# A residual block of a diffusion model: broken and unbroken PSUM writes in the plain products, and an opening cut in halves

## The chip, the cores and the metric

The kernel runs on one core of one Trainium2 chip. The metric is the time of one execution on the device, in microseconds (us), as the median of several runs. A core has five engines that the text names: TensorE (PE, matrix products; PEld is its loading of weights), VectorE (DVE), ScalarE (ACT), GpSimd (POOL) and SyncE (SP, which here only issues DMAs). Products land in PSUM, eight banks of 512 fp32 values in each of 128 partitions; DVE and ACT read them from there into SBUF.

## What is computed

Two images of 512 channels and 64 x 64 pixels go through group norm, silu and a 3 x 3 convolution, twice, with a time embedding added between, and the input added at the end:

```python
    h = conv3(_silu(gn(x, g1, be1)), w1)
    emb = _silu(t_emb) @ w_emb
    h = h + emb.reshape(B, C, 1, 1)
    h = conv3(_silu(gn(h, g2, be2)), w2)
    return x + h
```

`gn` has four groups of 128 channels, so that a group is exactly one block of 128 partitions; `conv3` pads with zeros and sums nine taps.

## The kernel before

**Tiling.** Channels are four blocks of 128 (`ct` for the input, `k` or `j` for the output). The work is eight chunks: layer 0 or 1, image 0 or 1, upper or lower half of the rows. A chunk has four units, one for each output block. A row of 64 pixels is stored as 32 even columns, one zero, 32 odd columns, so rows have a pitch of 65 elements (`RW`), and a plane (`PL`) has 8 rows.

**Fast convolution.** The rows of the 3 x 3 window are not multiplied one by one. Input rows are combined into six planes `s` (planes 4 and 5 by `rows_a`, planes 0 to 3 by `rows_b`, sums and scalings on DVE or ACT), each plane is multiplied with row-combined weights (`row_w`, called by `prep_w1` and `prep_w2`), and a unit combines the six results to output rows. Along columns a plane is either multiplied with the three column taps (`plain_mms`: products of 512 columns, 3 taps for each of 4 input blocks, all summed in one bank), or reduced once more along columns (`B_mms`, `A_mms`: products of 256 columns). Chunk 0 uses only plain products, chunks 1 to 3 use them for planes 1, 3, 4 and 5, chunks 4 to 6 for planes 4 and 5, chunk 7 for none: 1152 plain products and 1536 of width 256 in all.

**A plain product's patterns** (lines 780 to 791). The side taps (`kx` 0 and 2) read a plane as 8 runs of 64 elements and write the bank with the two halves of each row exchanged: `Ps(bank, 32, [[64, 8], [-32, 2], [1, 32]])`. The centre tap (`kx` 1) reads 16 runs of 32 elements and writes the bank without a break. `evac_o` and `evac_m` (lines 930 to 935) then read the bank without a break, on ACT.

**Order.** The kernel is not written in the order in which it runs. Every step is an operation with an engine, a price in us, and the memory it reads and writes; a planner (`Plan`) derives the dependences, simulates the five queues with these prices, and issues each engine's instructions in the order of that simulation. Within an engine the order is fixed from then on. `solve` makes priorities from the lengths of the paths behind each operation and then adds a list of seeded random offsets (`ORDER`); `boost` and `push` shift single operations.

**The opening** (lines 1120 to 1245). The first image's norm needs its statistics before any product can run. `stats0(ct)` takes them for one block: each half of the image by one of three ways, `CFG['st0']`: on DVE (`bn`: statistics instructions, their aggregation, two small steps), on ACT (a squaring with an accumulator, the sum by products with ones), or on PE. `gn_chain` sums over partitions by small fp32 products, then five small steps on DVE and a power on POOL (line 527) give scale and bias (lines 529 and 531). `silu` on ACT applies both to all 33 rows, `rows_a` makes planes 4 and 5 together, and their products for three output blocks (`opening`, banks 0 to 5) run while the other blocks' norms are made. Then come `rows_b`, the remaining products of unit 0, and the chunks. The row-combined weights of output block 0 and input block 0 are made on PE (`pe_w1`): 12 products with scaled identities (made by POOL, line 1201) and one evacuation. The other blocks' weights are made by `prep_w1` (two scalings on ACT, three 768-wide sums on DVE).

**Other parts touched.** `emb` makes the embedding on PE out of five loads of `w_emb`. `stats1` takes the second image's statistics on ACT during chunk 0. In a unit's end, `CFG['s']` names the engine of three scalings for each chunk (line 1019). `last_y` (line 1056) is the very last unit's end, on DVE.

Of the kernel before, what the change touches and what calls it, by code (L numbers as in the profile page):

```python
# [21 lines left out]
class Op:  # L22
    __slots__ = ("i", "eng", "cost", "lat", "fn", "preds", "succs", "name", "start", "slack", "sw", "boost")


ORDER = (2, (
    (194738957, 20, 15, 0.3),
    (101069860, -50, 500, 0.3),
    (792247291, 256, 60, 0.3),
    (343585110, 429, 120, 0.3),  # L30
    (204379228, 255, 30, 1),
    (228258273, 205, 30, 0.3),
    (909785710, 175, 15, 3),
    (736748984, 341, 30, 3),
    (920935792, 232, 15, 1),
    (771920438, 148, 30, 0.3),
    (603830373, 185, 60, 1),
    (465507377, 35, 15, 3),
    (12286073, 156, 15, 3),
    (538606607, 42, 15, 0.3),  # L40
    (581003105, 181, 60, 0.3),
    (15050380, 351, 120, 0.3),
    (657287205, 50, 30, 1),
    (104726034, 137, 60, 1),
    (1026753447, 57, 15, 0.3),
    (567570243, -16, 30, 1),
    (655024064, 49, 30, 0.3),
    (871214791, 61, 30, 3),
    (1017425442, 337, 30, 1),
    (41879747, 157, 120, 0.3),  # L50
    (6871566, 68, 15, 1),
    (894584394, 172, 15, 1),
    (297107780, 183, 60, 0.3),
    (207024721, 173, 60, 0.3),
    (908214038, 37, 30, 1),
    (122425277, 28, 30, 0.3),
    (791595493, 332, 15, 1),
    (223803721, 57, 15, 1),
    (904223640, 360, 15, 3),
    (301944938, 170, 120, 1),  # L60
    (380912920, 352, 60, 0.3),
    (625742557, 201, 30, 1),
    (907392232, 310, 15, 1),
    (117292907, 217, 60, 0.3),
    (948785046, 259, 15, 1),
    (731252551, 400, 15, 3),
    (676749781, 361, 15, 1),
    (521842705, 215, 60, 0.3),
    (955098089, 181, 15, 0.3),
    (956556455, 137, 15, 1),  # L70
# [3 lines left out]
class Plan:  # L74
# [118 lines left out]
    def solve(self, rounds=3):  # L193
# [15 lines left out]
        st, span = self._run(pris[k], False)  # L209
        st, pri = np.array(st), np.array(pris[k])  # L210
# [33 lines left out]
def _idx(off, dims):  # L244
# [27 lines left out]
    's': ((A_, A_, A_), (D_, D_, D_), (D_, A_, A_), (D_, D_, D_), (A_, A_, A_), (A_, A_, A_), (A_, A_, A_), (D_, A_, D_)),  # L272
    'oacc': (1,1,1,0,0,0,0,0),
    'np': 1,
    'st0': ('DA', 'DA', 'DP', 'PP'),
    'st1': 'AAAA',
    'warm': 9,
    'push': (40.0, 0.0, 0.0, 0.0),
    'wpe': (1, 0, 0, 0),
# [5 lines left out]
def kernel(  # L285
# [112 lines left out]
    def tt(out, a, b, op, name=""):  # L398
        pl.op("DVE", 0.075 + 0.000521 * out.n, lambda: nc.vector.tensor_tensor(out=out.ap, in0=a.ap, in1=b.ap, op=op),  # L399
              regs(a, b), regs(out), name)  # L400
# [5 lines left out]
    def act(out, a, func, scale=1.0, bias=None, acc=None, name=""):  # L406
        kw = {}
        rr, ww = [a], [out]
        sc = scale
        if isinstance(scale, R):  # L410
            rr.append(scale)
            sc = scale.ap
        if bias is not None:
            rr.append(bias)
            kw["bias"] = bias.ap
        if acc is not None:
            ww.append(acc)
            kw["accum_out"] = acc.ap
        if out.ap.dtype == F8:
            kw["saturate"] = False  # L420
        pl.op("ACT", (0.05 if a.reg[0] == "P" else 0.1) + 0.000833 * out.n + (0.09 if acc is not None else 0.0) + (0.18 if bias is not None else 0.0),
              lambda: nc.scalar.activation(out=out.ap, in_=a.ap, func=func, scale=sc, **kw), regs(*rr), regs(*ww), name)  # L422
# [18 lines left out]
    def mm(lst, name="", chain=True, slack=2.5, boost=0.0, warm=1.0):  # L441
        rr, ww, cost = [], [], 0.0
        for out, lhsT, rhs, st, sp in lst:
            rr += [lhsT, rhs]
            ww.append(out)
            cost += {512: 0.2222, 256: 0.109, 384: 0.166}.get(rhs.n, max(0.0715, rhs.n / 2330.0)) * warm
# [27 lines left out]
    EPSC = Fc(CT)  # L474

# [12 lines left out]
    nc.vector.memset(fs[:, EPSC:EPSC + CT], EPS)  # L488
    nc.gpsimd.tensor_tensor(out=fs[:, WARM:WARM + 1], in0=fs[:, WARM + 1:WARM + 2], in1=fs[:, NEGH:NEGH + 1], op=ALU.pow)
# [11 lines left out]
    def small(fn, r, w, name, cost=0.125):  # L501
        pl.op("DVE", cost, fn, regs(*r), regs(*w), name)

    def gn_chain(layer, b, ct, mes, name, SB=7, slack=5.0, n=1):
# [6 lines left out]
        lst.append((Ps(SB, n, [[1, n]]), cneg, F(EPSC, n), False, True))  # L511
# [6 lines left out]
        pl.op("DVE", 0.16, lambda: V.tensor_copy(out=F(tot, 2 * n).ap, in_=ps.ap), regs(ps), regs(F(tot, 2 * n)), name, boost=bo)  # L518
# [3 lines left out]
        else:  # L522
# [3 lines left out]
              [N], [N], name)  # L526
        pl.op("POOL", 0.85 if n == 1 else 1.9, lambda: nc.gpsimd.tensor_tensor(  # L527
            out=F(rs, n).ap, in0=N.ap, in1=F(NEGH, n).ap, op=ALU.pow), regs(N), regs(F(rs, n)), name)
        small(lambda: V.tensor_mul(out=S.ap, in0=F(rs, n).ap, in1=F(g, n).ap), [F(rs, n)], [S], name)
        if n == 1:  # L530
            small(lambda: V.scalar_tensor_tensor(  # L531
# [156 lines left out]
    def silu(c, ct):  # L688
        l, b, ch = chunks[c]
        ab = acur[(c, ct)]  # L690
        r0 = RW if ch == 0 else 0
        dims = [[RW, 33], [33, 2], [1, 32]]
# [6 lines left out]
    def rows_a(c, ct, w, keng, early):  # L699
# [10 lines left out]
        else:  # L710
            tt(v45, two(w, 0, 25), two(ab, 9, 17), SB_, nm)

# [63 lines left out]
    def plain_mms(bank, c, k, ct, s):  # L776
# [3 lines left out]
        for i, kx in enumerate((0, 2, 1)):  # L780
# [6 lines left out]
            if kx == 1:  # L787
                rhs, o = A(vo, [[RW, 8], [33, 2], [1, 32]]), Ps(bank, 0, [[1, 512]])
            else:
                rhs, o = A(vo + kx // 2, [[RW, 8], [1, 64]]), Ps(bank, 32, [[64, 8], [-32, 2], [1, 32]])  # L790
# [113 lines left out]
    def unit(c, k, opening=0):  # L904
# [25 lines left out]
        def evac_o(s, bank):  # L930
            act(A(OO[s - 4], [[RW, 8], [33, 2], [1, 32]]), Ps(bank, 0, [[1, 512]]), fid,
                scale=(0.25, 1.0)[s - 4], acc=acc(s), name=nm + f"o{s}")

        def evac_m(s, bank, i):
            act(M(s), Ps(bank, 0, [[1, 512]]), fid, scale=KAP[s], acc=i, name=nm + f"m{s}")

        def evac_pair(s, bank):
            act(M(s, 2, 1024), Ps(bank, 0, [[512, 2], [1, 512]]), ACT.Copy, scale=KAP[s], name=nm + f"m{s}")

# [43 lines left out]
        elif md == "0":  # L983
# [9 lines left out]
            evac_m(2, p2, acc(1))  # L993
            evac_m(0, p2 + 1, None)
# [61 lines left out]
    def last_y(c, k, M, SD, OS, OA, bank):  # L1056
# [16 lines left out]
        ts(M(1), M(0), 2.0, nm + "2")  # L1073
        tt(row(yb, 8, BF16), one(dx + 512), M(1), AD, nm + "y")
        ts(M(3), M(2), 4.0, nm + "4")
# [5 lines left out]
        ts(M(1), M(0), 8.0, nm + "8")  # L1081
# [48 lines left out]
    def bn(pieces, out, scale, name):  # L1130
        mv = Fc(2)
        V = nc.vector
        for i, d in enumerate(pieces):
# [6 lines left out]
        small(lambda: V.tensor_scalar(  # L1140
            out=out.ap, in0=F(mv, 2).ap, scalar1=scale, scalar2=None, op0=ALU.mult), [F(mv, 2)], [out], name)

    def stats0(ct):
# [24 lines left out]
        for h, base in enumerate((XB0[ct] + RW, XB1[ct])):  # L1168
            cold = 1.0
            if how[h] == "D":  # L1170
                me = Fc(2)
                bn([A(base + i * 416, [[1, 416]], BF16) for i in range(5)], F(me, 2), YF / HW, nm)
# [5 lines left out]
            else:  # L1178
                sq = Fc(1)
                act(A8(jk, YF), A(base, [[1, YF]], BF16), ACT.Square, scale=float(HW) ** -0.5, acc=F(sq), name=nm)  # L1180
                mes.append((sq, 1, 1))
        if "P" in how:
# [4 lines left out]
                out=j2.ap, in0=g.ap, scalar=1.0 / HW, in1=ident[:], op0=ALU.mult, op1=ALU.mult, accum_out=F(mg).ap),  # L1187
                regs(g), regs(j2, F(mg)), nm)
            mes.append((mg, 1, 1))
        if begun:  # L1190
            s1 = Fc(1)
            junk = A(MB + (ct % 2) * 512, [[1, 260]], BF16)
            act(junk, Ps(bk, 0, [[1, 260]]), ACT.Identity, scale=1.0 / (P * HW), acc=F(s1), name=nm)
            mes.insert(0, (s1, 0, 1))
        gn_chain(0, 0, ct, mes, nm, SB=bk, slack=0.0)

    IDS = {}
    for i, v in enumerate((-1.0, 2.0, -2.0, 4.0)):
        d = A(AB[0] + i * 128, [[1, 128]], BF16)
        IDS[v] = d  # L1200
        pl.op("POOL", 0.3, lambda d=d, v=v: nc.gpsimd.tensor_scalar(
            out=d.ap, in0=ident[:], scalar1=v, scalar2=None, op0=ALU.mult), (), regs(d), "ids")
    IDS[1.0] = cid

    def pe_w1(ct):

        nm = f"w1_0{ct}"
        d = A(RAW[ct % 2] + 1152, [[1, 384]], BF16)
        dma(d.ap, w1[0][:, 3072 + ct * 384:3072 + (ct + 1) * 384], [], [d], P * 768, nm)
        load_ur_ct(0, ct)  # L1210
        w0 = UREG[0] + 7168 + ct * 768
        lst = []
        for s, (c0, c2, c1) in enumerate(((1.0, 1.0, -1.0), (1.0, 4.0, -2.0), (1.0, 1.0, 1.0), (1.0, 4.0, 2.0))):
            for i, (cf, src) in enumerate(((c0, w0), (c2, w0 + 384), (c1, RAW[ct % 2] + 1152))):
                lst.append((Ps(s, 0, [[1, 384]]), IDS[cf], A(src, [[1, 384]], BF16), i == 0, i == 2))
        for i in range(0, 12, 3):
            mm(lst[i:i + 3], nm, chain=False, slack=0.0)
        act(A(UREG[0] + ct * 1792, [[128, 4], [512, 3], [1, 128]]), Ps(0, 0, [[512, 4], [128, 3], [1, 128]]), ACT.Copy, name=nm)

    for ct in range(CT):  # L1220
        if CFG["wpe"][ct]:
            pe_w1(ct)
    for ct in range(CT):
# [9 lines left out]
        silu(0, ct)  # L1233
        rows_a(0, ct, WB[ct % 3], CFG["k0"][ct], True)
        pl.push = 0.0
        for j in range(3):
            if j or not CFG["wpe"][ct]:
                load_ur_ct(j, ct)
            mm(plain_mms(2 * j, 0, j, ct, 4), "o")
            mm(plain_mms(2 * j + 1, 0, j, ct, 5), "o")  # L1240
        rows_b(0, ct, WB[ct % 3], CFG["t0"], True)
    for ct in range(CT):
        if not CFG["wpe"][ct]:
            prep_w1(0, ct)
# [5 lines left out]
    def stats1(ct):  # L1250
        nm = f"st1{ct}"
        me, mq = ME1 + ct, ME1 + CT + ct
        use_bn = CFG["st1"][ct] == "D"
        bk = 6 + ct % 2
        part = Fc(4)
        psum_ = Fc(4)
        pieces = []
        for i in range(4):
            pb = VB[0] + (ct * 4 + i) % 3 * VP + 3120
            d = A(pb, [[1, 1040]], BF16)  # L1260
            r0 = 1 + 16 * (i % 2)
            dma(d.ap, x[1, ct, i // 2][:, r0 * RW:(r0 + 16) * RW], [], [d], P * 2080, nm)
            if use_bn:
                pieces += [A(pb + 260 * q, [[1, 260]], BF16) for q in range(4)]
                continue
            if CFG["st1"][ct] == "A":
                act(A8(VB[0] + 3 * VP + 3120 + i % 2 * 520, 1040), d, ACT.Identity, scale=1.0 / HW, acc=F(psum_ + i), name=nm)
            else:
              mm([(Ps(bk, 0, [[1, 260]]), cone, A(pb + 260 * q, [[1, 260]], BF16),
# [167 lines left out]
```

## Time and profile before

| | |
|---|---|
| median of 8 runs | 464.47 us |
| lowest and highest run | 462.2 and 661.76 us |
| the profiled execution | 465.35 us |
| its span, first to last instruction | 463.6 us |
| granted TensorE clock, mean | 0.992 |
| PE, plain products of width 512 | 1152, 388 ns each |
| PE, products of width 256 | 1536, 273 ns each |
| DVE, 1040-wide sums | 179, 695 ns each |
| DVE, 1024-wide sums | 226, 691 ns each |
| ACT, 512-wide evacuations | 135, 603 ns each |
| ACT, silu of a block | 32, 2161 ns each |
| HBM traffic | 62.25 MB read, 31.32 MB written |

Products overlap in the pipeline, so a product's duration says less than the distance between the starts of two neighbours; a run of n products that takes T us, with d for the last one's own duration, has a pitch of (T - d)/(n - 1). Instructions of DVE and ACT overlap by less than 0.1 us as well. One outlying run of the eight (661.76) does not move the median.

### The profile page before, as it was taken

How to read it: one execution, taken by the hardware profiler on the slowest of the kernel's cores; microseconds unless marked ns; L12 is line 12 of the kernel's file. 1: busy time of each engine (PE TensorE's matmuls, PEld its weight loads, DVE VectorE, ACT ScalarE, POOL GpSimd, SP SyncE). 2: the span in 40 equal slices, each digit the busy share in tenths (PEclk: the TensorE clock that was granted, in tenths of full speed). 3: DMA queues.
4: the chain of work that ended last, by engine and by line, in shares of the span. 5: the costliest groups of instructions: out<-in, count | busy, mean ns of one | idle time of the engine just before them, and what ended most of it. 6: DMA issues, size and time to landing. Idle time of an engine off the chain costs nothing. (4 is left out here: it accounts for less than half of the span.)

```text
span 463.6 us, 8299 instructions
## 1 busy us (share of the span) xinstructions
PE 446.9 (96%) x2878; PEld 278.4 (60%) x2878; DVE 429.9 (93%) x847; ACT 396.0 (85%) x620; POOL 66.2 (14%) x94
## 2 busy tenths in 40 slices
PE   6989999999999999999999999999999999999992
PEld 4744444455555555555555566767666667788882
DVE  4998999929999999979899999998999999999997
ACT  5898999999999998689995798858999999767562
POOL 4120010103111221111010001113111101011211
PEclk9999999999999999999999999999999999999998
DMA  8982778869888587998998567866987645463934
GB/s 315 365 293 66 207 195 230 195 198 255 264 258 218 150 230 185 263 281 255 301 303 285 167 214 229 186 184 95 272 181 189 145 141 112 115 161 72 183 68 92
DMA packets 45977, 94.10 MB, mean 203 GB/s; under 512 B 7024, under 2 KB 18160, under 8 KB 45936
## 3 DMA queue, kind: packets, MB, share of 16 engines
q1 hardware_dynamic: 35712, 77.60, 50.5%
q0 software_dynamic: 9936, 15.98, 22.7%
q8 instruction: 22, 0.36, 0.3%
q14 instruction: 19, 0.16, 0.1%
q10 hardware_dynamic: 288, 0.01, 0.0%
HBM read 62.25 MB, written 31.32 MB: 202 GB/s over the span
## 5 line engine op out<-in xcount | busy, mean ns | idle before, releaser
L450 PE MATMUL psum<-ar 128*128 128x256 f16 (+2 forms) x2744 | 432.7, 320 | 2.4 <-ACT ar L422 1.2
L399 DVE TENSOR_TENSOR ar<-ar 128x1040 f16<-128x1040 f16 (+6 forms) x677 | 401.7, 658 | 14.9 <-ACT ar L422 11.1
L450 PEld LDWEIGHTS <-ar 128*128 128x128 f16 (+1 forms) x2780 | 268.1, 98 | 167.5 <-issue 5.7
L422 ACT ACTIVATE ar<-ar 128x384 bf16<-128x384 bf16 (+6 forms) x211 | 183.5, 911 | 13.0 <-DVE ar L399 9.7
L422 ACT ACTIVATE ar<-psum 128x512 f16<-128x512 f32 (+4 forms) x228 | 156.9, 723 | 37.5 <-PE psum L450 24.5
L422 ACT ACTIVATE ar<-ar,fs 128x2112 f16<-128x2112 bf16 (+1 forms) x32 | 69.0, 2161 | 4.0 <-DVE fs L531 2.3
L435 POOL DMA_DIRECT2D ar<-ar x30 | 30.8, 1043 | 182.5 <-DVE ar L399 109.3
L435 POOL DMA_DIRECT2D out_dram<-ar x15 | 18.1, 1208 | 104.1 <-DVE ar L399 101.4
L403 DVE TENSOR_SCALAR ar<-ar 128x512 f16<-128x512 f16 (+2 forms) x61 | 21.9, 372 | 0.4 <-ACT ar L422 0.4
L422 ACT ACTIVATION_READ_ACCUMULATOR ar<-psum 128x1 f32 x96 | 20.8, 216 | 0.0
L439 POOL MEMSET ar<- 128x65 f16 (+6 forms) x30 | 6.3, 245 | 71.9 <-DVE ar L399 28.4
L527 POOL TENSOR_TENSOR fs<-fs 128x1 f32<-128x1 f32 (+1 forms) x7 | 8.9, 1276 | 27.7 <-DVE fs L525 27.6
L422 ACT ACTIVATION_READ_ACCUMULATOR ar<-ar 128x1 f32 x50 | 10.2, 204 | 0.0
L1134 DVE BATCH_NORM_STATS2 fs<-ar 128x6 f32<-128x416 bf16 x15 | 8.1, 580 | 0.0
L450 PE MATMUL psum<-ar,ones_bf 128*128 128x260 bf16 x40 | 5.3, 275 | 2.5 <-DMA ar<-in_x_dram 1.7
L1276 DVE TENSOR_REDUCE fs<-fs 128x1 f32<-128x4 f32 x4 | 0.6, 152 | 6.8 <-ACT ar L422 6.8
L450 PEld LDWEIGHTS psum<-fs,ones_neg 128*128 128x128 f32 x42 | 5.7, 191 | 1.6 <-DVE ar L1186 0.7
L450 PEld LDWEIGHTS <-ones_bf 128*128 128x128 bf16 x40 | 3.8, 99 | 4.1 <-issue 2.6
L450 PE MATMUL psum<-fs,ones_neg 128*128 128x1 f32 (+3 forms) x42 | 5.3, 240 | 0.3 <-DVE ar L1186 0.2
L465 PE MATMUL psum<-ones_bf 128*128 128x512 bf16 x9 | 4.0, 631 | 1.1 <-DVE ones_bf L456 1.1
L450 PE MATMUL psum<-s_sb,ar 128*128 128x2 bf16 x36 | 1.5, 165 | 2.0 <-DMA ar<-in_w_emb_dram 2.0
L518 DVE COPY fs<-psum 128x2 f32<-128x2 f32 (+1 forms) x7 | 1.1, 156 | 2.3 <-PE psum L450 2.3
(47 smaller groups left out, 23.1 us busy)
## 6 DMA issues: line engine op xcount, KB each, us to landing
ar<-in_w_dram SPq DMA_DIRECT2D x32, 384.0 KB, 4.3
ar<-in_x_dram SPq DMA_DIRECT2D x16, 552.5 KB, 4.6
h_scr<-ar SPq DMA_DIRECT2D x16, 520.0 KB, 3.6
ar<-h_scr SPq DMA_DIRECT2D x16, 520.0 KB, 4.7
out_dram<-in_x_dram SPq DMA_DIRECT2D x30, 260.0 KB, 4.2
ar<-ar POOLq DMA_DIRECT2D x30, 260.0 KB, 4.8
out_dram<-ar POOLq DMA_DIRECT2D x15, 520.0 KB, 5.9
u_scr<-ar SPq DMA_DIRECT2D x16, 384.0 KB, 3.8
```

The costliest lines, as they stand in the source:

```text
L399: pl.op("DVE", 0.075 + 0.000521 * out.n, lambda: nc.vector.tensor_tensor(out=out.ap, in0=a.ap, in1=b.ap, op=op), regs(a, b), regs(out), name)
L403: pl.op("DVE", cost or 0.075 + 0.00026 * out.n, lambda: nc.vector.tensor_scalar(out=out.ap, in0=a.ap, scalar1=s, scalar2=None, op0=ALU.mul ...
L422: lambda: nc.scalar.activation(out=out.ap, in_=a.ap, func=func, scale=sc, **kw), regs(*rr), regs(*ww), name)
L435: lambda: eng.dma_start(out=out, in_=in_, **kw), regs(*r), regs(*w), name, lat=lat or (3.2 if sw else None), after=after, sw=sw)
L439: pl.op("POOL" if eng == "gpsimd" else "DVE", 0.08 + 0.0005 * out.n, lambda: e.memset(out.ap, v), (), regs(out), name)
L450: ins = nc.tensor.matmul(out.ap, lhsT=lhsT.ap, rhs=rhs.ap, start=st, stop=sp, skip_group_check=True)
L465: nc.tensor.matmul(psum[:, 0:512], lhsT=ones_bf[:], rhs=wr, start=True, stop=True, skip_group_check=True)
L518: pl.op("DVE", 0.16, lambda: V.tensor_copy(out=F(tot, 2 * n).ap, in_=ps.ap), regs(ps), regs(F(tot, 2 * n)), name, boost=bo)
L527: pl.op("POOL", 0.85 if n == 1 else 1.9, lambda: nc.gpsimd.tensor_tensor(out=F(rs, n).ap, in0=N.ap, in1=F(NEGH, n).ap, op=ALU.pow), regs(N ...
L1134: pl.op("DVE", 0.07 + 0.00104 * d.n, lambda d=d, i=i: V.bn_stats(out=F(BNS + 6 * i, 6).ap, in_=d.ap), regs(d), regs(F(BNS + 6 * i, 6)), name)
L1276: pl.op("DVE", 0.1, lambda: nc.vector.reduce_sum(out=F(me).ap, in_=F(psum_, 4).ap, axis=AX.X), regs(F(psum_, 4)), regs(F(me)), nm)
```

## The change

- **Plain products.** The side taps now write the bank without a break. The centre tap reads the even columns of all eight rows and then the odd ones, and writes one half of each row at a time. The bank then holds the halves of each row exchanged, and the evacuations of plain products read it so (`Pw`).
- **Opening.** `silu`, the scaling and the sums of `rows_a` are cut into two parts (`rows_h`), one for plane 4 and one for plane 5, with the products of each behind its part. The DMAs of the outer taps' weights (`load_ur_ct`) are at no raised priority.
- **Norm chain of the first image.** Statistics are kept per half of the image, and the factor one half moves into the copy out of PSUM (and into `EPS2`), so that a scaling in `bn` falls away. The product with the gain moves from DVE to POOL, right behind the power, and the bias from DVE to ACT (`bact`).
- **Weights of block (0, 0).** `pe_w1` and its identities are gone; `prep_w1` makes them.
- **Engines.** Chunk 0's three scalings of each unit go from ACT to DVE. Three scalings of `last_y` go from DVE to ACT.
- **Order.** The list of random offsets is another one, and a table `NUDGE` shifts the priority of 35 named groups of operations. The price of a 512-wide product is 0.2195 instead of 0.2222.
- `stats1` loses branches that are not taken; what it does is the same.

```diff
             if kx == 1:
-                rhs, o = A(vo, [[RW, 8], [33, 2], [1, 32]]), Ps(bank, 0, [[1, 512]])
+                rhs, o = A(vo, [[33, 2], [RW, 8], [1, 32]]), Ps(bank, 32, [[-32, 2], [64, 8], [1, 32]])
             else:
-                rhs, o = A(vo + kx // 2, [[RW, 8], [1, 64]]), Ps(bank, 32, [[64, 8], [-32, 2], [1, 32]])
+                rhs, o = A(vo + kx // 2, [[RW, 8], [1, 64]]), Ps(bank, 0, [[1, 512]])
...
-            act(A(OO[s - 4], [[RW, 8], [33, 2], [1, 32]]), Ps(bank, 0, [[1, 512]]), fid,
+            act(A(OO[s - 4], [[RW, 8], [33, 2], [1, 32]]), Pw(bank), fid,
...
-        def evac_m(s, bank, i):
-            act(M(s), Ps(bank, 0, [[1, 512]]), fid, scale=KAP[s], acc=i, name=nm + f"m{s}")
+        def evac_m(s, bank, i, plain=True):
+            act(M(s), Pw(bank) if plain else Ps(bank, 0, [[1, 512]]), fid, scale=KAP[s], acc=i, name=nm + f"m{s}")
...
+        Pw = lambda bank: Ps(bank, 32, [[64, 8], [-32, 2], [1, 32]])
...
-    's': ((A_, A_, A_), (D_, D_, D_), (D_, A_, A_), (D_, D_, D_), (A_, A_, A_), (A_, A_, A_), (A_, A_, A_), (D_, A_, D_)),
+    's': ((D_, D_, D_), (D_, D_, D_), (D_, A_, A_), (D_, D_, D_), (A_, A_, A_), (A_, A_, A_), (A_, A_, A_), (D_, A_, D_)),
...
+        if half:
+            def power():
+                nc.gpsimd.tensor_tensor(out=N.ap, in0=N.ap, in1=F(NEGH, n).ap, op=ALU.pow)
+                return nc.gpsimd.tensor_tensor(out=S.ap, in0=N.ap, in1=F(g, n).ap, op=ALU.mult)
+
+            pl.op("POOL", 0.95, power, regs(N, F(g, n)), regs(N, S), name)
+            if CFG["bact"]:
+                return act(B, T0, ACT.Identity, scale=S, bias=F(g + CT), name=name)
...
-    def silu(c, ct):
+    def silu(c, ct, rows=None):
         l, b, ch = chunks[c]
         ab = acur[(c, ct)]
-        r0 = RW if ch == 0 else 0
-        dims = [[RW, 33], [33, 2], [1, 32]]
+        a, n = rows or (1 if ch == 0 else 0, 33)
+        r0 = a * RW
+        dims = [[RW, n], [33, 2], [1, 32]]
...
+    def rows_h(c, ct, w, keng, h):
+        ab = acur[(c, ct)]
+        nm = f"row{c}{ct}"
+        one = lambda base, r: A(base + r * RW, [[1, PL]])
+        a, n = ((0, 17), (17, 16))[h]
+        scal(keng, A(w + a * RW, [[1, n * RW]]), A(ab + a * RW, [[1, n * RW]]), 4.0, f"k{c}{ct}")
+        r, s, z = ((9, 1, 0), (17, 26, 25))[h]
+        tt(one(w, r), one(ab, s), one(w, r), SB_, nm)
+        tt(one(w, z), one(w, z), one(ab, r), SB_, nm)
+        return tt(A(vplane(c, ct, 4 + h), [[1, PL]]), one(w, z), one(w, r), AD, nm)
...
-        silu(0, ct)
-        rows_a(0, ct, WB[ct % 3], CFG["k0"][ct], True)
+        for h in range(2):
+            silu(0, ct, ((1, 16), (17, 17))[h])
+            rows_h(0, ct, WB[ct % 3], CFG["k0"][ct], h)
+            for j in range(3):
+                if h == 0:
+                    pl.push = 0.0
+                    load_ur_ct(j, ct)
+                    pl.push = CFG["push"][ct]
+                mm(plain_mms(2 * j + h, 0, j, ct, 4 + h), "o")
         pl.push = 0.0
-        for j in range(3):
-            if j or not CFG["wpe"][ct]:
-                load_ur_ct(j, ct)
-            mm(plain_mms(2 * j, 0, j, ct, 4), "o")
-            mm(plain_mms(2 * j + 1, 0, j, ct, 5), "o")
         rows_b(0, ct, WB[ct % 3], CFG["t0"], True)
     for ct in range(CT):
-        if not CFG["wpe"][ct]:
-            prep_w1(0, ct)
+        prep_w1(0, ct)
...
-        ts(M(1), M(0), 2.0, nm + "2")
+        scal("ACT", M(1), M(0), 2.0, nm + "2")
...
-        ts(M(3), M(2), 4.0, nm + "4")
+        scal("ACT", M(3), M(2), 4.0, nm + "4")
...
-        ts(M(1), M(0), 8.0, nm + "8")
+        scal("ACT", M(1), M(0), 8.0, nm + "8")
```

## The prediction

> **What bounds the kernel now.** I first read the busy shares of the page, then busy time by stage, then the gaps of TensorE (PE), then the chain of waits at the end. The page's first part:
>
> ```profile
> PE 446.9 (96%) x2878; PEld 278.4 (60%) x2878; DVE 429.9 (93%) x847; ACT 396.0 (85%) x620; POOL 66.2 (14%) x94
> ```
>
> PE and VectorE (DVE) are both nearly full, so saving on one pays only where the other can follow. Busy time by stage shows where that is (columns: stretch, its length, then busy us of PE, weight load, DVE, ACT, POOL):
>
> ```profile
> 18.00:33.00 15.00, 12.72 (x110) 7.59 (x108) 13.92 (x42) 14.92 (x22) 3.02 (x3) 0.99 0.91 316
> 33.00:93.00 60.00, 60.00 (x265) 26.01 (x263) 57.25 (x117) 57.47 (x117) 5.28 (x5) 0.97 0.67 178
> 93.00:136.00 43.00, 42.83 (x244) 23.73 (x243) 33.25 (x71) 42.97 (x83) 5.90 (x5) 1.00 0.84 246
> 136.00:226.00 90.00, 90.00 (x515) 50.23 (x514) 83.14 (x181) 82.78 (x151) 15.15 (x18) 1.00 0.84 229
> 226.00:320.00 94.00, 93.27 (x604) 58.96 (x603) 93.40 (x166) 75.26 (x107) 11.53 (x19) 1.00 0.74 220
> ...
> 340.00:446.00 106.00, 104.54 (x818) 79.71 (x816) 105.62 (x174) 85.20 (x101) 13.90 (x18) 1.00 0.58 138
> ```
>
> From 33 to 226 PE has no room and DVE has some 19 us. From 226 on DVE is full too. So time won before 226 moves everything earlier, time won on PE later is worth little. ACT is full from 18 to 136. Before 33 PE is not full; its timeline there:
>
> ```profile
> 29.46 0.96 PE L450 MATMUL psum<-s_sb,ar 128*128 128x2 bf16 x24
> 32.39 0.61 PE L450 MATMUL psum<-s_sb,ar 128*128 128x2 bf16 x12 [1.97 <-DMA ar<-in_w_emb_dram]
> 32.87 5.32 PE L450 MATMUL psum<-ar 128*128 128x512 f16 x16
> ```
>
> PE stands 2 us behind the embedding's weights, and the next products are slow: 16 take 5.32 us, where 16 at the steady pitch below take 15 x 0.2225 + 0.386 = 3.72. That is 1.6 us more, the granted clock of the stretch being 0.97. Only 36 of the opening's 72 products were done by then. At the end the chain of waits reads (start, length):
>
> ```profile
> 422.38 24.08 PE psum L450 x218
> ...
> 448.05 1.29 DVE ar L399 x2
> ...
> 456.16 0.20 DVE ar L403
> 456.36 1.00 DVE ar L399 x3
> ```
>
> So the tail is DVE work, 0.20 us for a scaling and 0.33 for a 512-wide sum.
>
> **The plain products.** All 1152 products of width 512 are touched: 288 in chunk 0, 576 in chunks 1 to 3, 288 in 4 to 6. Two lines of the PE timeline give pitches:
>
> ```profile
> 51.82 10.40 PE L450 MATMUL psum<-ar 128*128 128x512 f16 x46
> ...
> 384.29 3.44 PE L450 MATMUL psum<-ar 128*128 128x256 f16 x30
> ```
>
> The last one of each takes 386 and 273 ns, so the pitches are (10.40 - 0.386)/45 = 222.5 ns and (3.44 - 0.273)/29 = 109.2 ns. The Trainium skill (TensorE: Matmul & The Clock Gate, Back-to-back issue gap) gives N/2.4 + 2.5 ns: 109.2 for 256, which the row meets, and 215.8 for 512, which it misses by 6.7 ns. Something in the access pattern costs 6.7 ns, in all 1152.
>
> What? A rule speaks against the change: PSUM — Partial Sum Buffer (Specifications) says that any non-contiguous pattern slows matmuls significantly, and the centre tap, whose write is unbroken now, becomes the broken one. By that rule alone two side taps gain 6.7 and the centre tap loses about as much: mean -2.2 ns. The rows disagree with it twice. The 256-wide run above writes 32-wide pieces 64 apart, and is at 109.2. And the centre tap writes unbroken today and pays like the side taps: the starts inside a group of three differ by 1 ns. What it has is a read in 16 pieces of 32, so for it the read is the cost, 6.7/16 = 0.4 ns a piece. The side taps read 8 pieces of 64: by the same price 3.3 of their 6.7 ns, and the rest is their write, which steps back by 32 in each row. I take that: side taps 219.2, centre tap unchanged, mean -2.2 ns. Ends: side taps pay by the read alone, no gain (and +6.7 on the centre tap, mean +2.2, if its newly broken write adds to its read); or by the write alone, side taps 215.8, mean -4.4. The planner's new price (0.2195, -2.7 ns) lies between.
>
> Worth: some 710 plain products run between 33 and 226: 710 x 2.2 ns = 1.6 us. Of the 400 later ones perhaps a quarter counts, 0.2, since DVE is full. Together **1.8 us**.
>
> Evacuations now read the broken form on ACT. Evacuations that write stepped rows and such that write unbroken rows both take 0.60 us in chunk 0, so I price the stepped read at nothing; the cover, if it had a cost, is ACT's 40 us of idle time after 226.
>
> **The opening.** Moved onto DVE, at start-to-start cost (1040-wide sum 0.61, 520-wide 0.33, 768-wide 0.47, scaling of 512 0.20, of 2145 0.63, small ones 0.13):
> - rows in halves: six 520-wide sums for three 1040-wide (+0.15) and one more scaling's start (+0.07), four times: +0.9;
> - weights of block (0,0) by vector sums instead of PE: three 768-wide, +1.4. It leaves PE with 12 products fewer and ACT with 1.45 - 2 x 0.41 less. Two DMAs leave the head of SP's queue, where they stood ahead of two x loads;
> - chunk 0's scalings from ACT: 12 x 0.20 = +2.4; ACT loses 12 x 0.63 = 7.6 where it was full;
> - away: three scalings after the statistics (-0.4), and four times the norm's product and sum (-1.1).
>
> Net +3.2 us on DVE, 2.6 of it before chunk 1. DVE's own waits before chunk 1 are 5.3 us (1.74, 0.57, 0.44, 1.66 and small ones), and its last wide sum before chunk 1's first 256-wide products (PE, 93.2) ends at 91.0. So DVE allows chunk 1 at 91.0 + 2.6 - 5.3 = 88.3 at best, which is **4.9 us earlier**, no more.
>
> What PE can win: a first half plane needs 1.1 us less of silu, 0.3 less scaling and 3 x (0.61 - 0.33) less of sums, so it is ready about 2.2 us sooner after each norm. The products of ct 2 and 3 then stand ready where PE now waits (2.1 us with its sequencer) and runs slow (1.6). That is 3.7; I take **3.0**, since DVE must find nearly all of it in its own waits, and the pitch takes 0.5 of the same allowance. Ends: 0 and 4.4.
>
> The norm chain: POOL multiplies after its power, ACT makes the bias. SBUF — State Buffer (Who interferes with whom) says that a GpSimd instruction that reads SBUF contends with two-input vector instructions, which speaks against a second POOL step. The rows agree: the power takes 0.58 us alone, 1.0 to 1.4 beside vector sums. The step it replaces is no better: power's end at 24.10, bias ready at 25.46, queued behind sums on DVE. By 0.58 on POOL and 0.25 on ACT the chain gains 0.5, by 1.0 it gains 0.1; inside the 3.0.
>
> **Tail.** Three scalings of 0.20 leave DVE for ACT, idle there after 454.9. On ACT each takes 0.63 (the row of 512-wide copies) and DVE must wait for it, behind no other work of ACT; sums that need no scaling can stand between. Between -0.6 and +0.4; I take **-0.4**.
>
> **Order.** All priorities change. PE's waits after 226 (0.9 at 303.5, 1.4 at 370.5, 0.6 at 421.5) are what a new order can win or lose: -2 to +2, taken at **-0.4**.
>
> **Sum**: 1.8 + 3.0 + 0.4 + 0.4 = 5.6 us. Against the profiled execution (465.35, span 463.6) 459.75; the median of the runs is 0.88 lower, so 458.9.
>
> **Rivals.**
> 1. The pitch does not move (the side taps pay for their read): 1.8 less won, 460.7. For it: the centre tap's row. Against it: that tap has twice the pieces at the same pitch.
> 2. All goes at its best: pitch 218.1 (3.1 + 0.3), opening 3.8, tail 0.6, later waits down by 2: 9.8 us, 454.7. Against it: DVE full from 226 on.
> 3. Slower: DVE's added 2.6 us lie on the path. If the order leaves its waits before 91 as they are, chunk 1's planes are ready at 93.6 and later with each norm step queued behind six sums instead of three; PE then stands from 92 to 95, and as at 32.87 a stand of 2 us brings 1.6 us of slow products: +1.8 +1.6, less 1.3 of pitch later, 466.6. It decides from the point where the recovered waits are under about 1 us. For it: DVE at 57.25 of 60. Against it: 6.8 us of DVE wait at 92.9 on ACT, which loses work.
>
> **Chances.** Forecast 0.52, rival 1 0.20, rival 2 0.15, rival 3 0.08, near no change by smaller losses of order 0.05. A measurement here tells 0.3% (1.4 us) from nothing: faster means under 463.1. Faster 0.87, same 0.06, slower 0.07. The range 454.5 to 463.0 takes in rival 1 and the edge of rival 2.
>
> **What would show it.** Right: 512-wide runs at about 220 ns, uneven by tap; no 2 us wait on the embedding's weights and no 427 ns products after 30; PE on chunk 1's 256-wide products near 89.5; DVE still full from 226. Wrong: pitch at 222.5 in all three taps; a DVE-ended wait of PE near 90; the gain of 90 gone by 340.

## The result, and the profile after

The changed kernel takes 458.72 us (median of 11 runs) where the kernel before takes 463.96 in the same session: a ratio of 0.9896, 95% interval 0.9876 to 0.9916. The forecast was 458.9. The sum is right; its parts are not, as the profile shows at once. The profiled execution took 458.81 us, with a span of 456.8.

The busy shares of the page, after:

```profile
PE 445.1 (97%) x2866; PEld 276.7 (61%) x2866; DVE 432.7 (95%) x865; ACT 392.5 (86%) x620; POOL 63.0 (14%) x94
```

DVE is busy 2.8 us longer in a span 6.8 us shorter, and ACT 3.5 us less. By stage (columns as in the prediction):

```profile
18.00:33.00 15.00, 14.06 (x113) 8.42 (x112) 12.12 (x39) 12.16 (x19) 2.46 (x6) 0.92 0.74 262
33.00:93.00 60.00, 60.00 (x285) 26.78 (x284) 59.86 (x127) 59.78 (x122) 5.21 (x5) 1.00 0.71 199
93.00:136.00 43.00, 43.00 (x248) 23.81 (x247) 41.73 (x97) 42.85 (x80) 7.95 (x7) 1.00 0.86 243
136.00:226.00 90.00, 90.00 (x516) 49.79 (x514) 86.51 (x186) 84.27 (x151) 14.60 (x19) 1.00 0.86 242
226.00:320.00 94.00, 94.00 (x615) 59.70 (x614) 89.75 (x157) 76.03 (x106) 10.98 (x18) 1.00 0.76 219
340.00:446.00 106.00, 106.00 (x845) 82.15 (x844) 104.79 (x178) 81.48 (x99) 12.80 (x16) 1.00 0.59 133
```

The third row is the one to look at. Between 93 and 136 DVE did 33.25 us of work before and does 41.73 now (7 more 512-wide scalings are some 2 us of that, the rest is other work, done sooner than before); from 226 to 320 it is no longer full, and PE is at 94.00 of 94 and 106.00 of 106, without a wait. The waits of DVE from 93 to 136, before:

```profile
DVE fs L1276 <- ACT ar L422: 6.8, 1, 6.8
DVE fs L1280 <- ACT ar L422: 1.5, 1, 1.5
DVE ar L399 <- ACT ar L422: 1.2, 2, 0.9
```

and after (this is its only line):

```profile
DVE ar L423 <- ACT ar L446: 1.1, 2, 0.7
```

Two lines of PE's timeline answer to the pitch, one to the end of the opening:

```profile
51.73 10.61 PE L474 MATMUL psum<-ar 128*128 128x512 f16 x47
...
32.56 3.49 PE L474 MATMUL psum<-ar 128*128 128x512 f16 x15 [0.94 <-DVE ar L423]
```

The mean pitch of a plain product is (10.61 - 0.385)/46 = 222.3 ns, against 222.5. The new patterns moved PE by 0.2 ns x 1152 = 0.25 us. The second line says that PE's 2 us on the embedding's weights have become 0.94 us on DVE, and that the products after it run at full pitch.

A ledger of the two profiled executions, from the starts of the same products in both traces (us; PE's last product ends at 455.18 and 449.75, DVE's last instruction at 460.33 and 453.76):

| place | before | after | won |
|---|---|---|---|
| start of chunk 1's 256-wide products | 93.21 | 91.51 | 1.7 |
| PE's waits at 101.8 and 108.0 | 0.5 | 0 | 0.5 |
| PE's waits at 303.5, 370.5, 421 to 422 and 433.8 | 3.0 | 0 | 3.0 |
| pitch of 1152 products | 222.5 ns | 222.3 ns | 0.25 |
| PE's last product to DVE's last instruction | 5.15 | 4.01 | 1.1 |

These make 6.6 us; the two profiled executions are 6.5 apart, the medians 5.2, as the profiled execution of the kernel before lies 1.4 us above its median. The opening's row varies from run to run, as told below.

### The profile page after: what moved, and what is told of

Its sections match the earlier page's. It is cut to its first block, busy times and chain, and to the rows that moved or that the text cites. A ratio compares the mean times of both kernels' runs of the same rounds, so it can differ in the third digit from the quotient of the medians.

```text
span 456.8 us, 8314 instructions
## 1 busy us (share of the span) xinstructions
PE 445.1 (97%) x2866; PEld 276.7 (61%) x2866; DVE 432.7 (95%) x865; ACT 392.5 (86%) x620; POOL 63.0 (14%) x94
## 5 line engine op out<-in xcount | busy, mean ns | idle before, releaser
L423 DVE TENSOR_TENSOR ar<-ar 128x1024 f16<-128x1024 f16 (+6 forms) x692 | 403.5, 649 | 10.2 <-ACT ar L446 6.5
L446 ACT ACTIVATE ar<-psum 128x512 f16<-128x512 f32 (+3 forms) x227 | 157.2, 719 | 42.2 <-PE psum L474 32.8
L446 ACT ACTIVATE ar<-ar 128x512 f16<-128x512 f16 (+6 forms) x204 | 180.3, 921 | 8.5 <-DVE ar L423 6.8
L446 ACT ACTIVATE ar<-ar,fs 128x2112 f16<-128x2112 f16 (+3 forms) x36 | 70.4, 1964 | 0.6 <-DMA ar<-h_scr 0.3
L427 DVE TENSOR_SCALAR ar<-ar 128x512 f16<-128x512 f16 (+4 forms) x74 | 24.9, 349 | 0.0
L474 PE MATMUL psum<-ar,ones_bf 128*128 128x260 bf16 x40 | 6.8, 332 | 1.8 <-DVE fs L545 0.9
L567 POOL TENSOR_TENSOR fs<-fs 128x4 f32<-128x4 f32 x3 | 4.0, 1348 | 22.4 <-DVE fs L555 22.4
L559 POOL TENSOR_TENSOR fs<-fs 128x1 f32<-128x1 f32 x4 | 3.0, 745 | 22.5 <-DVE fs L555 22.5
```

The lines of the kernel that those rows point to most:

```text
L423: return pl.op("DVE", 0.075 + 0.000521 * out.n, lambda: nc.vector.tensor_tensor(out=out.ap, in0=a.ap, in1=b.ap, op=op), regs(a, b), regs(o ...
L427: pl.op("DVE", cost or 0.075 + 0.00026 * out.n, lambda: nc.vector.tensor_scalar(out=out.ap, in0=a.ap, scalar1=s, scalar2=None, op0=ALU.mul ...
L474: ins = nc.tensor.matmul(out.ap, lhsT=lhsT.ap, rhs=rhs.ap, start=st, stop=sp, skip_group_check=True)
L559: nc.gpsimd.tensor_tensor(out=N.ap, in0=N.ap, in1=F(NEGH, n).ap, op=ALU.pow)
```

## The experiments: the plain products

The theory here: the new patterns are worth nothing as they stand, since the centre tap loses what the side taps win. In the trace the starts of neighbours are 218.5 ns apart behind a side tap and 230.0 behind a centre tap, where before all were within 1 ns of 222.5. The price list of the prediction (0.4 ns for each piece read) gives the side taps nearly right, but not the centre tap. Four kernels take it apart. In all of them DVE, ACT, POOL and SP keep their queues, and PE its order, so only patterns differ (in the third also the number of products).

**Old patterns in the new kernel.** The three lines of the diff that concern patterns, undone.

> The changed kernel with the old patterns of plain products and their evacuations, everything else and its order as changed. Ledger theory (the new patterns move only 0.2 ns a product, 222.5 to 222.3; the gain came from the opening, from later waits and from the tail): all taps at 222 to 223 ns, span 456.8 to 457.4, ratio to the kernel before 0.990. Rival (the patterns carry the 1.8 us that the prediction gave them, for example through the evacuations): span 458.6 or more, ratio 0.993.

Measured: 222.5 ns for all taps; ratio 0.9881 (0.985 to 0.9913), 458.36 us. From the 72nd opening product to the end of PE it takes 0.3 us longer than the changed kernel, as the pitch says; its profiled span is nevertheless 455.3, because its opening was 1.8 us shorter. The ledger theory holds: the patterns are worth 0.25 us, too little for the medians to show.

**Centre tap unbroken in its write.**

```diff
-                rhs, o = A(vo, [[33, 2], [RW, 8], [1, 32]]), Ps(bank, 32, [[-32, 2], [64, 8], [1, 32]])
+                rhs, o = A(vo + 33, [[RW, 8], [-33, 2], [1, 32]]), Ps(bank, 0, [[1, 512]])
```

> The changed kernel, the centre tap writing the bank unbroken as the side taps do, its read taking the odd half of each row first (start 33, step -33); same order of all instructions. If the centre tap's 230 ns are its newly broken write on top of its broken read: centre tap back at 222 ns, side taps 218.5, mean 219.8, and chunk 3's end 1.8 us earlier than in the changed kernel; span 455.0 if DVE follows, 456.5 if DVE's full stretch from 226 eats it. If the read alone sets it (reading halves out of order costs): centre tap stays at 230, span 456.8.

Measured: centre tap 229.2 ns, ratio 0.989 (0.9859 to 0.9921). The first expectation misses. A write in one piece brings 0.8 ns of the 7.5, so nearly all of the extra cost isn't the write.

**Centre tap as two products.**

```diff
-                rhs, o = A(vo, [[33, 2], [RW, 8], [1, 32]]), Ps(bank, 32, [[-32, 2], [64, 8], [1, 32]])
+                for q in range(2):
+                    lst.append((Ps(bank, 32 * (1 - q), [[64, 8], [1, 32]]), w, A(vo + 33 * q, [[RW, 8], [1, 32]]), False, ct == CT - 1 and q == 1))
+                continue
```

> The changed kernel, the centre tap as two products of 256 columns, one for each half (8 runs of 32 read, 8 runs of 32 written 64 apart), prices and order kept. If a broken read costs per run: 2 x (109.2 + 8 x 0.4) = 225 ns for the two, mean 220.7, so 1.1 us by chunk 3's end. If the cost of 230 comes from both sides broken in one product: the two still pay it, 230. If it comes from the jump between halves alone: 218.4, mean 218.5, 2.6 us by chunk 3's end. Span between 454.5 and 457.

Measured: 116.0 and 114.9 ns, together 230.9; ratio 0.9921 (0.9897 to 0.9945). A 256-wide product with the same write but an unbroken read has 109.2 (the prediction's row), so 8 read pieces that lie 33 elements apart cost 6.3 ns, 0.8 a piece, twice the 0.4 that the prediction took. The sum is the 230 of the second expectation, but its reason (both sides broken) is not it: the centre tap had 229.2 with an unbroken write too.

**Centre tap row by row, both sides broken.**

```diff
-                rhs, o = A(vo, [[33, 2], [RW, 8], [1, 32]]), Ps(bank, 32, [[-32, 2], [64, 8], [1, 32]])
+                rhs, o = A(vo, [[RW, 8], [33, 2], [1, 32]]), Ps(bank, 32, [[64, 8], [-32, 2], [1, 32]])
```

> The changed kernel, the centre tap row by row (read even then odd half of each row, write stepping back by 32 in each row) in place of one column half at a time. If breaks on both sides add up whatever their order: 230 ns as in the changed kernel, span 456.8. If the step back in the write is what costs: about 236 ns, 1152/3 x 6 = 2.3 us more on PE, 1.4 of it before DVE is full, span 458.2.

Both expectations miss, to the good: the centre tap is at 222.5 and the side taps at 219.2, mean 220.3. The durations of plain products from 52 to 62 us (minimum/median/maximum, in ns) tell the same without any working; the kernel before, the changed one, and this one:

```profile
L450 PE MATMUL psum<-ar x46: 386/386/387, 51.8 to 61.8; 128*128 128x512 f16 x46
```

```profile
L474 PE MATMUL psum<-ar x47: 379/381/392, 51.7 to 61.9; 128*128 128x512 f16 x47
```

```profile
L474 PE MATMUL psum<-ar x48: 382/383/386, 51.6 to 62.0; 128*128 128x512 f16 x48
```

So the order of the read is what costs: 16 pieces read nearly in the order of memory (gaps of one element at most) take 222.5 ns, the same 16 pieces with jumps of half a row or a row take 229 to 230, whatever the write does. The side taps' write, stepping back in each row, cost 3 to 4 ns (222.5 with it, 218.5 to 219.2 without). A write that only steps forward, 64 apart, costs nothing (the 256-wide products: half of them write so, half without a break, and from 93 us on nearly all start 108 to 111 ns apart). That a step back costs nothing behind 16 read pieces (222.5 with and without it) would fit a product that pays for the worse of its two sides; that was not tried by itself.

This is the version with the least PE work, 2.0 ns x 1152 = 2.3 us under the changed kernel. Its time is 459.32 us, ratio 0.9895 (0.9856 to 0.9934): the same as the changed kernel's. Counted from chunk 1's start PE has gained 1.1 us on the changed kernel when, in chunk 5, it stands for ACT:

```profile
329.77 1.69 PE L474 MATMUL psum<-ar 128*128 128x256 f16 x14
331.99 1.26 PE L474 MATMUL psum<-ar 128*128 128x512 f16 x5 [0.52 <-ACT ar L446]
```

From chunk 1's start to PE's end it takes 357.75 us, the changed kernel 358.24. Of 1.8 us of pitch in that stretch (900 products), 0.5 are left.

## The experiments: where the 5 us came from

**Without the late random offsets.** `ORDER`'s 13 entries that begin at 250 us or later are passed over.

```diff
         for seed, t0, w, sg in moves:
+            if t0 >= 250:
+                continue
```

> The changed kernel without the 13 random offsets of the order that begin at 250 us or later; everything before about 250 us as changed. If PE's waits after 226 (2.9 us in the kernel before, none in the changed one) went away by the tuned order: 2 to 4 us of PE waits come back after 250, all ended by ACT or DVE, with PE's wide products of chunk 1 starting where they do in the changed kernel; ratio to the kernel before 0.994 to 0.998. Rival (they went because DVE and ACT arrive less loaded): PE waits after 250 stay under 0.5 us, ratio 0.990.

Measured: PE waits 0.2 us after 250, DVE's tail behind PE 5.2 us in place of 4.0; ratio 0.9929 (0.9902 to 0.9956). The rival holds for PE: the late waits did not go by a tuned late order. In the trace the late offsets are worth about 1 us, in the tail; the intervals of the two ratios overlap.

**Last unit's scalings on DVE.** `scal("ACT", ...)` back to `scal("DVE", ...)` three times in `last_y`.

> The changed kernel with the last unit's three scalings back on DVE; PE's order unchanged. From PE's last product to DVE's last instruction the kernel before takes 5.15 us and the changed one 4.01. If the three scalings are that: 4.6 to 5.2 us here, span 0.6 to 1.1 longer, about 457.6 at the changed kernel's opening. Rival (the rest of the tail's order did it): 4.0 to 4.3 us, nothing in the span.

Measured: 4.69 us from PE's end to DVE's end, 0.68 more than in the changed kernel; ratio 0.9867 (0.9829 to 0.9905), too wide to see 0.7 us. So the three scalings are 0.7 of the tail's 1.1 us, what three rows of 0.20 on DVE promised, with nothing lost to waiting for ACT.

**Chunk 0's scalings on ACT.**

```diff
-    's': ((D_, D_, D_), (D_, D_, D_), (D_, A_, A_),
+    's': ((A_, A_, A_), (D_, D_, D_), (D_, A_, A_),
```

> The changed kernel with chunk 0's twelve scalings back on ACT. If moving them was needed because ACT is full from 18 to 136 us: ACT gets 7.6 us more there, PE waits on ACT between 90 and 140 for 2 us or more, and DVE's wait for ACT near 93 to 100 comes back (6.8 us in the kernel before); ratio 0.994 or more. Rival (ACT's excess is only work of the second image's statistics, which nobody needs before chunk 2): PE waits under 0.5 us as in the changed kernel, ratio 0.990.

Measured: 477.62 us (the profiled execution took 473.75), ratio 1.0254 (1.0196 to 1.0312): slower than the kernel before. DVE's wait for ACT is back between 93 and 136,

```profile
DVE fs L1290 <- ACT ar L446: 3.9, 2, 1.9
DVE ar L423 <- ACT ar L446: 3.3, 3, 2.6
```

and PE's waits from 33 us on, none in the changed kernel, are

```profile
PE psum L474 <- DVE ar L423: 8.7, 6, 4.3
PE psum L474 <- ACT ar L446: 3.4, 2, 1.8
PE psum L474 <- DVE fs L548: 0.5, 1, 0.5
```

**The opening in one piece.** `silu` over 33 rows and `rows_a` for both planes; the second half's five steps are empty places of no cost.

```diff
-            silu(0, ct, ((1, 16), (17, 17))[h])
-            rows_h(0, ct, WB[ct % 3], CFG["k0"][ct], h)
+            if h == 0:
+                silu(0, ct)
+                rows_a(0, ct, WB[ct % 3], CFG["k0"][ct], True)
+            else:
+                for eng, nm in (("ACT", "silu"), ("DVE", "k"), ("DVE", "row"), ("DVE", "row"), ("DVE", "row")):
+                    pl.op(eng, 0.0, lambda: None, (), (), f"{nm}0{ct}")
```

> The changed kernel with silu and the sums of planes 4 and 5 of chunk 0 in one piece again (four empty places stand in for the second half's steps, so that the random offsets fall on the same operations). If the halves bring the opening's gain: the 36th plain product of the opening and chunk 1's first 256-wide product come 1 to 2 us later than in the changed kernel (30.6 and 91.5), ratio 0.993. Rival (they only add 0.9 us to DVE, and the gain of the opening is the order of the embedding and the norms): both come within 0.5 us or earlier, ratio 0.990 or less.

Measured: 469.3 us, ratio 1.0099 (1.0066 to 1.0131); chunk 1 starts at 97.3. The 36th product is not late (30.25 against 30.56), the next ones are:

```profile
30.48 1.04 PE L474 MATMUL psum<-s_sb,ar 128*128 128x2 bf16 x36
36.56 4.00 PE L474 MATMUL psum<-ar 128*128 128x512 f16 x9 [5.04 <-DVE ar L423]
```

PE stands 5 us for the planes of the third block, and the starts of nine of the following products lie 427 ns apart.

Both of these are confounded. The list of offsets and `NUDGE` came with the changed kernel; when a price or an engine changes, the planner's simulation moves, and the same offsets may do harm. The expectations named ratios of 0.993 and of 0.994 or more, and both kernels are slower than the kernel before. So the last four kernels have no offsets and no `NUDGE` at all: the planner's own order (`boost` and `push` stay), for four structures.

**The changed kernel, plain order.**

> The changed kernel with the planner's own order: no shifts from the table, no random offsets. If the gain is in the structure (what runs where, and in which pieces): about 0.985 to 0.99 of the plain version of the kernel before, at whatever level. If the gain is in the tuned order: the two plain versions take the same time within 0.5%, and both are 2% or more slower than their tuned ones.

**The kernel before, plain order.**

> The kernel before with the planner's own order, no random offsets. Its difference to the tuned one is what the old list of offsets was worth; expected 2 to 4% slower (474 to 483 us), with PE waits before 45 us and after 300 us. If the offsets are worth nothing, 464.5.

**Plain order, chunk 0's scalings on ACT.**

> The plain order with chunk 0's twelve scalings back on ACT. Tuned offsets can't be spoiled here. If the scalings are what cost 15 us: 10 us or more above the plain changed kernel, with PE waiting on ACT or DVE before 140. If that was a spoiled order: within 3 us of it, either way.

**Plain order, the opening in one piece.**

> The plain order with the opening's silu and sums in one piece. If the halves themselves win: the plain changed kernel starts its 36th opening product and chunk 1's 256-wide products 1 to 3 us earlier than this one. If the 10 us were a spoiled order: both within 1 us of each other.

The last three columns are from one profiled execution each:

| plain order | median us | ratio to the kernel before (tuned) | chunk 1 starts | PE ends | PE's waits after 226 |
|---|---|---|---|---|---|
| changed | 463.1 | 0.9968 (0.995 to 0.9985) | 91.30 | 451.98 | 1.0 |
| before | 471.48 | 1.0155 (1.0124 to 1.0185) | 95.05 | 459.83 | 4.1 |
| changed, scalings on ACT | 469.02 | 1.0109 (1.0092 to 1.0125) | 93.17 | 459.58 | 3.9 |
| changed, opening whole | 469.34 | 1.0126 (1.0083 to 1.0169) | 94.23 | 457.94 | 3.9 |

In the same order, the stretch from 93 to 136 us (columns as in the prediction):

```profile
93.00:136.00 43.00, 42.59 (x242) 23.30 (x241) 40.15 (x92) 43.00 (x81) 6.73 (x6) 1.00 0.90 253
93.00:136.00 43.00, 42.56 (x242) 23.56 (x241) 33.44 (x75) 42.97 (x84) 6.03 (x5) 1.00 0.82 238
93.00:136.00 43.00, 41.14 (x237) 22.77 (x236) 34.69 (x81) 43.00 (x85) 5.74 (x5) 1.00 0.81 234
93.00:136.00 43.00, 43.00 (x247) 23.73 (x245) 39.45 (x96) 42.62 (x82) 8.40 (x7) 1.00 0.86 244
```

The gain is in the structure: without any tuning the changed kernel is 8.4 us faster than the kernel before, more than the 5.2 with tuning, because the old list of offsets had won more (1.0155 to 1, about 7 us, less than the 2 to 4% expected) than the new list and table (0.9968 to 0.9896, about 3). And the two parts are real: the scalings on ACT cost 5.9 us (expected: 10 or more, or within 3, so neither), the whole opening 6.2. In the tuned kernel the ratios make them 16.6 us (1.0254 against 0.9896) and 9.4 us (1.0099): some 10 and 3 of these were a spoiled order. The two parts are not additive: together they would be 12 us of 8.4, and other parts of the change (the weights of block (0, 0), the norm chain, the priority of the DMAs) were not undone alone.

The rows tell the scalings' part without any tuning: with them on ACT, DVE does 34.69 us of work between 93 and 136, as in the kernel before (33.44); without them 40.15. Its waits for ACT at the small sums of the second image's statistics go the same way: 7.3 us in the kernel before, 6.9 with the scalings on ACT, 1.5 in the changed kernel.

How the whole opening loses shows first in PE's timeline of the plain order, in one piece and in halves:

```profile
29.65 1.04 PE L474 MATMUL psum<-s_sb,ar 128*128 128x2 bf16 x36
34.18 11.11 PE L474 MATMUL psum<-ar 128*128 128x512 f16 x43 [3.49 <-DVE ar L423]
```

```profile
34.85 0.24 PE L474 MATMUL psum<-s_sb,ar 128*128 128x2 bf16 x4
35.92 9.26 PE L474 MATMUL psum<-ar 128*128 128x512 f16 x41 [0.83 <-DVE ar L423]
```

In one piece PE waits 3.5 us, and the run after it has 43 products in 11.11 us, 1.4 us over its pitch. In halves there are products to do all along, the wait is 0.8 us, and 41 take 9.26, which is the full pitch. So in this pair the halves win both the wait and the slow products behind it. The expectation is met in one half: chunk 1 starts 2.9 us earlier, but the 36th opening product does not (29.41 against 29.42). And this is half of the loss only: from chunk 1's start to PE's end the whole opening takes another 3.0 us, about as much as PE's waits after 226 grow (1.0 to 3.9), though DVE hardly waits between 93 and 136 (39.45). Why these come back was not tried.

## Why the prediction was right, and where it was not

- **Plain products, 1.8 us: wrong, 0.25.** The step that failed is the sentence "I take that: side taps 219.2, centre tap unchanged, mean -2.2 ns". The side taps are at 218.5. The centre tap isn't unchanged: 230.0, since the price of a read piece was taken as one number for all reads, and the change alters how far apart the pieces lie. The end that it named for this tap (+6.7) was right in size, but for another reason: it put it on the newly broken write, which is hardly it (229.2 with an unbroken write, 222.5 row by row with a write that is broken in every row). Rival 1, that the pitch does not move, came true for the mean, but not for its reason: both taps moved, against each other.
- **What pitch is worth after 226, a quarter: right in kind.** The row-by-row kernel has the pitch that the prediction took. In its trace PE has won 0.6 us on the changed kernel between chunk 1's start and 226, and 0.5 at its end, so nothing is left of what it won later. The time does not show it (an interval of 1.8 us to each side).
- **Evacuations in broken form at nothing: right.** The 135 evacuations take 603 ns each in both profiles, and with old patterns throughout the time is the same.
- **The opening, 3.0 us: mis-sized, 1.7 in the profiled pair.** One half of the mechanism is as told: products of later blocks are ready where PE stood. The other half, the 1.6 us of slow products, did not go away in the profiled pair, it moved. The granted clock, the third number from the end, was low after 33 us in the kernel before (first pair of rows) and from 18 to 24 us in the changed one (second pair):

```profile
18.00:24.00 6.00, 6.00 (x48) 3.91 (x46) 5.40 (x19) 5.92 (x12) 1.52 (x2) 1.00 0.85 289
33.00:42.00 9.00, 9.00 (x35) 3.58 (x33) 8.97 (x17) 7.46 (x15) 0.00 (x0) 0.82 0.19 56
```

```profile
18.00:24.00 6.00, 6.00 (x33) 3.18 (x31) 4.23 (x14) 5.97 (x9) 0.22 (x2) 0.80 1.05 398
33.00:42.00 9.00, 9.00 (x49) 4.05 (x48) 9.00 (x23) 9.00 (x24) 0.00 (x0) 1.00 0.41 135
```

Seven products start 427 ns apart in each, from 33.25 us before and from 17.13 us after. Chunk 1's start in the changed kernel and five others with its opening order is 91.5, 89.8, 91.5, 90.2, 90.5 and 90.7, so 1.7 to 3.4 us before 93.2. The spread is how many slow products fall at 17 us (7, 0, 8, 7, 1 and 2, in the same order) and when the first product starts (16.4 to 17.3 us). So how much the opening wins changes from execution to execution of the same order. From 18 us to chunk 1 DVE held PE once, for 0.94 us: rival 3 fell.
- **The norm chain: POOL's second step was overpriced.** It takes 0.19 us in the median, 0.37 at most, not 0.58 to 1.0. Its row was that of the power, which is another function.
- **Tail, 0.4: 1.1.** The three scalings are 0.7 of it, just beyond the far end given (0.6, three rows of 0.20). The order has its part: without the late offsets the tail is 5.2 us again, although the scalings are on ACT; without any offsets it is 5.44 before and 4.78 after.
- **Order, 0.4: 3.5, and it was mostly no matter of order.** The prediction saw DVE wait 6.8 us for ACT at 92.9, and used it only as an argument against rival 3. It is the main entry. DVE, which works in order, stood behind a small sum of the second image's statistics, which ACT made late because it was full (42.97 of 43 us). With twelve scalings fewer on ACT, DVE's waits for ACT from 93 to 136 go from 9.5 to 1.1 us, it does 8.5 us more work there, and from 226 to 320, where the prediction called it full and took that for a sign of being right, it has room (89.75 of 94). PE's 3.0 us of late waits and the 0.5 near 105 go with it. Undoing the scalings alone brings waits back on both sides of 226, in the tuned and in the plain order. They are not the only part, for the late waits also come back with the opening whole (3.9 us in the plain order), and the order takes the last 1.0. That the chain runs through DVE's lead is read from the busy rows; no run isolated it.

The forecast time came out by luck: 1.55 + 1.3 us too much on the first two entries met some 3.8 too little on the last two. The ends given hold the measured value for the first two, not for the tail (-0.6) and the order (-2).

## What to carry to other kernels

A wait in the middle of the kernel, on an engine that is full later, can cost time at the end, though PE does not stand while it lasts: it is lead that is missing there. Here 8.4 us less of such waits came with 3.5 us less of PE's. Follow what an engine gives up (7.6 us of scalings on ACT) to whoever waits for it, as carefully as what another takes on. When one product has several access patterns, give each a pitch of its own, and ask of a pattern not only how many pieces it has but how far apart they lie. And where the order was tuned by a search, compare structures in the untuned order: tuned against detuned made one part look nearly three times its size.

## What the runs showed of the hardware

- A plain product's pitch depends on how it reads: unbroken 109.2 ns for 256 columns; eight pieces of 32 with gaps of 33 elements 115 to 116. For 512 columns: 8 pieces of 64 one element apart 218.5 to 219.2, 16 pieces of 32 at most one element apart 222.5, the same 16 in an order that jumps 229 to 230. No plain product reads without a break, so the price from zero is not shown.
- Writing 32-wide pieces of a bank 64 apart cost nothing that shows (108 to 111 ns, as the unbroken writes of 256 columns); stepping back in every row cost a side tap 3 to 4 ns, and the centre tap, which reads 16 pieces, nothing (222.5 with and without).
- In the opening, stands of PE of 1.97, 1.94, 3.49, 4.26 and 5.04 us (kernel before, tuned and plain; plain whole opening; scalings on ACT; whole opening) were followed by 7, 10, 6, 5 and 9 products 427 ns apart, nearly twice the pitch, 1 to 2 us on top of the wait. The length of the stand alone does not decide it: stands of 2.04 us at 383 us (whole opening) and 2.59 us at 416 us (plain, scalings on ACT) were followed by none at a granted clock of 1.00, and the seven slow products of the changed kernel came behind stands of 0.86 and 0.58 us.
